# A routed expert stage on one core: the weight splits of a small tile's expert moved into the full tile ahead of it

## The chip, the cores and the metric

The kernel runs on one core of one Trainium2 chip. The metric is the device time of one execution in microseconds, the median of several runs; three runs of the kernel before stand below. One more execution was taken with the hardware profiler, and every row shown here is from that one.

## The reference

Attention, a gated feed-forward layer, and then a layer of eight experts of which each token uses one. The change touches the last layer alone:

```python
N, D, E, F = 896, 768, 8, 1024
logits = x @ w_gate + modality_bias[modality_id]
e_idx = np.argmax(logits, axis=1)
...
for e in range(E):
    mask = e_idx == e
    if not mask.any():
        continue
    h = np.maximum(x[mask] @ w1[e], 0.0)
    out[mask] = gate_w[mask, None] * (h @ w2[e])
```

With the inputs of the test, three experts get tokens: expert 2 has 463, expert 6 has 406 and expert 0 has 27.

## The kernel before

The experts' layer works through tiles of 128 token slots, numbered L from 0. Which expert a tile belongs to is computed on the chip, so the program holds for each tile L of 3 and above two bodies in an If with an Else: `tiny` for an expert's remainder of few tokens, and `full`. Tiles of 7 and above stand inside a further If on the count of tiles. Here the tiles are: 0 to 3 expert 2, all full; 4 expert 6, tiny with 22 tokens; 5 to 7 expert 6, full; 8 expert 0, tiny with 27 tokens; then the end.

`full` computes with weights that are split into a high and a low part (`ra`, made from the raw weights `r1f` of w1 and `r2f` of w2, which lies in the buffer `fa`). One chunk of a split is a cast on ACT (the high part: L795 for w1, L801 for w2) and a subtraction on DVE (the low part: L796 and L802). There are 6 chunks for w1 and 8 for w2. `mm1` (L838) is the product with w1, in two halves of 512 columns, and L915 the product with w2 (called mm2 here). `tiny` reads the raw weights: its product with w1 is L938 and that with w2 is L964, with transposes (L831, L950) and copies (L952) between.

While a tile runs, it prepares what is two tiles ahead: `onehots` (L723, L727 and seven times L731, on DVE) makes the matrices P, seven small matmuls (L744) and some small DVE operations (L746 to L760) turn these into row indices, and `gather` (L807, GpSimd) brings the rows. Rows that an index puts out of range are skipped. Each tile ends with a scaling by the gate, half on ACT and half on DVE (L924 and L925 in `full`, L971 and L972 in `tiny`), and a scatter of the rows (L927, L973).

When the next tile belongs to a new expert, `switch_w1(L)` at the end of tile L, in an If on the register flag_next, splits w1 and the first four chunks of w2, and issues the load of the w1 of the expert after that into `r1f` (a DMA with a condition, on SP). `switch_w2` in the middle of a full tile splits the other four chunks and loads `r2f`. For an expert that begins with a tiny tile, flag_next is set at that tiny tile: here at tile 4, for expert 6. The flags are rows of an integer tile `regs`; a register load (L785, a TENSOR_LOAD) stands on each engine that takes part in an If. Every engine runs the branches, each over its own list of instructions.

Engines take their instructions in program order. Nothing in this part is ordered by a table: the order is that of the code.

Of the kernel before, what the change touches and what calls it, by code (L numbers as in the profile page):

```python
# [458 lines left out]
class Route:  # L459
    def __init__(self, nc, tc, args, k, pool):  # L460
        self.nc, self.tc, self.a, self.k = nc, tc, args, k
        self.p = pool
        t = lambda n, s, d=F32: pool.tile(s, d, name=n)
        self.bsel = t("bsel", [128, NT7, E8])
        self.oh = t("oh", [128, NT7, E8])
        self.ohb = t("ohb", [128, NT7, E8], BF16)
        self.R = t("R", [128, NT7 + 1, E8], BF16)
        self.sums = t("sums", [128, NT7])
        self.rank = t("rank", [128, NT7])
        self.cols = t("cols", [128, NT7, 5], BF16)  # L470
        self.slot = t("slot", [128, NT7])
        self.regp = t("regp", [128, 1], I32)
        self.regs = t("regs", [128, 80], I32)
        self.idx = t("idx", [128, 16], I32)
        self.idxg = t("idxg", [128, 16], I32)
        self.idc = t("idc", [128, 16], I32)
        self.gate = t("gate", [128, 16])
        self.e0 = t("e0", [128, E8])
        self.c0 = t("c0", [128, 2])
        self.trib = t("trib", [128, 128], BF16)  # L480
        self.lgs = {}
        self.oneb = t("oneb", [128, 128], BF16)
# [169 lines left out]
    def flags(self, wk):  # L652
        nc, k = self.nc, self.k
        V = nc.vector
        w = lambda n, s: wk.tile(s, F32, name=n)
        n, gt, nt, base = self.fin
        rf = w("rf", [128, 80])
        V.memset(rf, 0.0)
        pos, act, ev = w("pos", [128, E8]), w("act", [128, E8]), w("ev", [128, E8])
        nact = w("nact", [128, 1])  # L660
        er = k[:, C_E:C_E + E8]
        V.tensor_reduce(out=rf[:, 0:1], in_=nt, op=ALU.add, axis=AX.X)
        V.tensor_scalar(out=rf[:, 0:1], in0=rf[:, 0:1], scalar1=2.0, scalar2=None, op0=ALU.add)
        V.tensor_reduce(out=pos, in_=gt, op=ALU.add, axis=AX.X)
        V.tensor_scalar(out=act, in0=n, scalar1=0.0, scalar2=None, op0=ALU.is_gt)
        V.tensor_tensor(out=ev, in0=act, in1=self.e0, op=ALU.mult)
        V.tensor_tensor(out=act, in0=act, in1=ev, op=ALU.subtract)
        V.tensor_reduce(out=nact, in_=act, op=ALU.add, axis=AX.X)
        V.scalar_tensor_tensor(out=ev, in0=pos, scalar=1.0, in1=er, op0=ALU.is_equal, op1=ALU.mult,
                               accum_out=rf[:, 1:2])  # L670
        V.tensor_scalar(out=rf[:, 2:3], in0=nact, scalar1=0.5, scalar2=None, op0=ALU.is_gt)
        V.tensor_copy(self.regs[:, 0:3], rf[:, 0:3])
        self.fl = (rf, pos, act, nact)
        v1 = self.tiny
        sT = [128, NL - TINY0, E8]
        Lt = k[:, C_L + TINY0:C_L + NL].unsqueeze(2).to_broadcast(sT)
        qa = w("qa", sT)
        self.ts = ts = w("ts", [128, NL])
        V.tensor_tensor(out=qa, in0=base.unsqueeze(1).to_broadcast(sT), in1=Lt, op=ALU.is_equal)
        V.tensor_tensor(out=qa, in0=qa, in1=v1.unsqueeze(1).to_broadcast(sT), op=ALU.mult)  # L680
        V.tensor_reduce(out=ts[:, TINY0:], in_=qa, op=ALU.add, axis=AX.X)
        V.tensor_copy(rf[:, 64 + TINY0:64 + NL], ts[:, TINY0:])

    def flags2(self, wk):
        nc, k = self.nc, self.k
        V = nc.vector
        w = lambda n, s: wk.tile(s, F32, name=n)
        n, gt, nt, base = self.fin
        rf, pos, act, nact = self.fl
        er = k[:, C_E:C_E + E8]  # L690
        sL = [128, NL, E8]
        Lr = k[:, C_L:C_L + NL].unsqueeze(2).to_broadcast(sL)
        bb = base.unsqueeze(1).to_broadcast(sL)
        ab = act.unsqueeze(1).to_broadcast(sL)
        q, q2, kc, kn = w("q", sL), w("q2", sL), w("kc", [128, NL]), w("kn", [128, NL])
        v1 = self.tiny
        bs, bn = w("bs", [128, E8]), w("bn", [128, E8])
        V.tensor_tensor(out=bs, in0=base, in1=v1, op=ALU.add)
        V.tensor_tensor(out=bn, in0=nt, in1=v1, op=ALU.is_gt)
        V.tensor_tensor(out=bn, in0=bn, in1=act, op=ALU.mult)  # L700
        V.tensor_tensor(out=q, in0=bs.unsqueeze(1).to_broadcast(sL), in1=Lr, op=ALU.is_equal)
        V.tensor_tensor(out=q, in0=q, in1=bn.unsqueeze(1).to_broadcast(sL), op=ALU.mult)
        V.tensor_reduce(out=rf[:, 16:16 + NL], in_=q, op=ALU.add, axis=AX.X)
        V.tensor_tensor(out=q2, in0=bb, in1=Lr, op=ALU.is_le)
        V.tensor_tensor(out=q2, in0=q2, in1=ab, op=ALU.mult)
        V.tensor_reduce(out=kc, in_=q2, op=ALU.add, axis=AX.X)
        V.tensor_scalar(out=kn, in0=kc, scalar1=1.0, scalar2=None, op0=ALU.add)
        V.tensor_tensor(out=q, in0=pos.unsqueeze(1).to_broadcast(sL), in1=kn.unsqueeze(2).to_broadcast(sL),
                        op=ALU.is_equal)
        V.tensor_tensor(out=q, in0=q, in1=er.unsqueeze(1).to_broadcast(sL), op=ALU.mult)  # L710
        V.tensor_reduce(out=rf[:, 32:32 + NL], in_=q, op=ALU.add, axis=AX.X)
        V.tensor_scalar(out=rf[:, 48:48 + NL], in0=kc, scalar1=nact[:, 0:1], scalar2=None, op0=ALU.is_lt)
        V.tensor_copy(self.regs[:, 16:64 + NL], rf[:, 16:64 + NL])

    def onehots(self, L, wk, part):
        nc, k = self.nc, self.k
# [21 lines left out]
    def index_first(self, wk, pp, name="px"):  # L738
        nc = self.nc
        V = nc.vector  # L740
        L, nt, P = self.P
        ps = pp.tile([128, 512], F32, name=name)
        for t in range(nt):
            nc.tensor.matmul(ps[:, :5], P[:, t], self.cols[:, t], start=(t == 0), stop=(t == nt - 1))  # L744
        s = wk.tile([128, 8], F32, name="ixs", bufs=2)
        V.tensor_copy(s[:, 0:5], ps[:, :5])  # L746
        V.scalar_tensor_tensor(out=s[:, 5:6], in0=s[:, 0:1], scalar=4096.0, in1=s[:, 1:2], op0=ALU.add, op1=ALU.add)  # L747
        V.tensor_scalar(out=self.idc[:, L:L + 1], in0=s[:, 5:6], scalar1=float(NTOK - 1), scalar2=None, op0=ALU.min)
        return L, s

    def index_rest(self, Ls):
# [11 lines left out]
class Moe2:  # L763
# [93 lines left out]
        nc.vector.tensor_tensor(out=lo, in0=v, in1=hi.bitcast(F32), op=ALU.subtract)  # L857
        self.hhl[hf] = (hi, lo)

    def fetch(self, raw, name, L, lf=None):  # L860
        if lf is None:
            lf = self.val(self.R.regs, 48 + L, 1, self.SP)
        e = self.val(self.R.regs, 32 + L, E8 - 1, self.SP)
        self.nc.sync.dma_start(raw, self.src(name, e), cond=lf, cond_hint=True)

    def switch_w2(self, L):
        with self.tc.If(self.flag > 0):
            for c in range(4, NFC):
                self.split_w2(self.r2f[:, c], c)
            self.fetch(self.r2f, "w2", L)  # L870

    def switch_w1(self, L):
        if L >= 1 and L + 1 < NL:
            with self.tc.If(self.flag_next > 0):  # L874
                for c in range(ND):
                    self.split_w1(self.r1f[:, c], c, 0, 2)
                self.fetch(self.r1f, "w1", L + 1)
            with self.tc.If(self.flag_next > 0):
                for c in range(4):
                    self.split_w2(self.r2f[:, c], c)  # L880
# [6 lines left out]
    def full(self, L, call):  # L887
# [5 lines left out]
        ps = [self.ph.tile([128, 512], F32, name="ph") for _ in range(2)]  # L893
        self.mm1(ps[0], 0, 0, 5)
        call("mid0")
        self.mm1(ps[0], 0, 5, ND)
        self.relu(ps[0], 0)
        call("mid1")
# [32 lines left out]
    def tiny(self, L, G):  # L931
# [29 lines left out]
        for c in range(C):  # L961
            for k in range(G):
                for g in range(G):
                    nc.tensor.matmul(y[W * g:W * g + W, 0:D2], ht[:, c, W * k:W * k + W],  # L964
                                     self.r2f[:, C * k + c, D2 * g:D2 * g + D2],
                                     start=(c == 0 and k == 0), stop=(c == C - 1 and k == G - 1))
        self.fetch(self.r2f, "w2", L, self.flag)
        self.switch_w1(L)
        yo = wk.tile([128, DM], F32, name="ysb", bufs=2)
        o = D2 // 2  # L970
        nc.scalar.activation(yo[:, 0:o], y[:, 0:o], AF.Copy, scale=R.gate[:, L:L + 1])  # L971
# [4 lines left out]
            in_offset=None, bounds_check=G * NTOK - 1, oob_is_err=False)  # L976

    def load_flag(self, L):
        self.flag_next = self.val(self.R.regs, 16 + L + 1, 1)

    def body(self, L, hooks):
        tc, R = self.tc, self.R
        call = lambda name: hooks.get((L, name), lambda: None)()
        more = L + 1 < NL
        if L >= 2 and more:
            self.load_flag(L)
        if L < TINY0:
            self.full(L, call)
        else:
            sm = self.val(R.regs, 64 + L, 1)  # L990
            with tc.If(sm > 0) as cmp:
                self.tiny(L, 4)
            with cmp.Else():
                self.full(L, call)
        call("end")
        if more:
            if L >= 1:
                self.flag = self.flag_next
            if L + 1 < NT7:
                self.body(L + 1, hooks)  # L1000
            else:
# [7 lines left out]
def build(nc, tc, a):  # L1009
    with ExitStack() as es0:  # L1010
# [246 lines left out]
        def mid3_1():  # L1257
# [4 lines left out]
            e = M.val(R.regs, 14, E8 - 1, M.SP)  # L1262
            nc.sync.dma_start(M.r2f, M.src("w2", e), cond=has, cond_hint=True)

        def end1():
            M.NT = M.val(R.regs, 0, NL)
        hooks = {(0, "start"): start0, (0, "mid1"): mid1, (0, "mid2"): mid2, (0, "mm2"): mm2, (0, "mid3"): mid3,
                 (1, "mid0"): mid0_1, (1, "mid2"): lambda: R.onehots(3, wk, False), (1, "mm2"): lambda: R.flags2(wk), (1, "mid3"): mid3_1, (1, "end"): end1}
        M.body(0, hooks)


# [63 lines left out]
```

## Time and profile before

| what | value |
| --- | --- |
| median of 3 runs | 627.27 us (626.29 to 630.08) |
| profiled execution | 626.63 us, of which the span of the profile is 624.9 us |
| TensorE busy | 96% of the span |
| DVE, ACT, GpSimd busy | 67%, 37%, 23% of the span |
| mean granted TensorE clock | 0.985 of full speed |

A busy share counts instructions that occupy the engine; branches, register loads and DMA issues count as idle time. The experts' layer takes the last part of the span: tile 3's second half, tile 4 and the first part of tile 5 lie between 530 and 560 us, and the last tile ends near 616 us.

### The profile page before, as it was taken

What the parts mean: (1) busy time and instruction counts of PE and PEld (TensorE: products, weight loads), DVE (VectorE), ACT (ScalarE), POOL (GpSimd) and SP (SyncE); (2) the same over time, 40 slices, a digit from 0 to 9 for tenths busy, and PEclk for the clock granted to TensorE, in tenths of its full rate; (3) what the DMA queues carried; (4) which work ended last, traced back from release to release, by engine and by line L of the source; (5) the groups of instructions that cost most, each with busy time, mean ns of one, the idle gap of its engine ahead of it and who ended that gap; (6) DMA issues with size and microseconds to landing.
All of it is one profiled execution on the core that took longest, in us unless ns stands there. A gap on an engine that the chain in (4) does not pass through costs nothing. (4 is left out here: it accounts for less than half of the span.)

```text
span 624.9 us, 16865 instructions
## 1 busy us (share of the span) xinstructions
PE 598.6 (96%) x6843; PEld 497.7 (80%) x6843; DVE 416.1 (67%) x993; ACT 234.0 (37%) x544; POOL 143.4 (23%) x243
## 2 busy tenths in 40 slices
PE   8789999999999999999999999999999999979993
PEld 3346666666778999999999979999998888769982
DVE  4478787878856878777777555987759833593322
ACT  4376676766652211111111252212364222361221
POOL 3477666767700000000000015000100101101101
PEclk9799999999999999999999999999999999979998
DMA  7677638656322654444455003310490661156102
GB/s 225 177 193 189 187 114 206 177 180 171 119 64 72 231 188 167 152 152 160 171 178 201 0 1 116 140 50 26 175 335 1 252 254 53 48 225 259 48 31 66
DMA packets 38178, 89.89 MB, mean 144 GB/s; under 512 B 12208, under 2 KB 15596, under 8 KB 38076
## 3 DMA queue, kind: packets, MB, share of 16 engines
q1 hardware_dynamic: 24060, 64.60, 30.7%
q0 software_dynamic: 14016, 23.95, 13.0%
q8 instruction: 62, 1.02, 0.7%
q14 instruction: 40, 0.33, 0.2%
HBM read 69.88 MB, written 5.70 MB: 121 GB/s over the span
## 5 line engine op out<-in xcount | busy, mean ns | idle before, releaser
L111 POOL DMA_DIRECT2D G<-S x156 | 92.2, 609 | 18.9 <-issue 7.8
L1131 PE MATMUL y<-ra,gh 128*128 128x384 f32 x324 | 70.6, 340 | 0.0
L392 ACT CAST whi<-wdec 128x768 fp32r<-128x768 f32 x24 | 20.0, 835 | 124.2 <-DVE wdec L376 116.9
L139 ACT ACTIVATE e<-t,st 124x448 f32<-124x448 f32 x90 | 56.2, 633 | 15.1 <-DVE st L130 15.1
L838 PE MATMUL ph<-ra,xsh 128*128 128x512 f32 x168 | 54.9, 409 | 5.0 <-ACT ra L801 4.5
L130 DVE TENSOR_REDUCE st<-t 124x1 f32<-124x448 f32 x90 | 52.1, 619 | 11.2 <-PE t L122 8.4
L165 PEld LDWEIGHTS o<-Wp,e 60*56 60x56 f32 (+1 forms) x2880 | 48.2, 132 | 13.7 <-issue 12.5
L1131 PEld LDWEIGHTS y<-ra,gh 128*128 128x128 f32 x324 | 56.8, 188 | 0.6 <-issue 0.3
L122 PE MATMUL t<-G,wpre 60*64 60x448 f32 x360 | 53.4, 555 | 3.9 <-DMA G<-S 3.6
L165 PE MATMUL o<-Wp,e 60*56 60x60 f32 (+1 forms) x2880 | 54.0, 221 | 2.4 <-issue 1.4
L189 PEld LDWEIGHTS v<-A2T,vt 120*64 120x64 f32 x672 | 33.6, 136 | 26.6 <-DVE st L148 18.3
L1107 POOL TENSOR_TENSOR ra<-wo,ra 128x768 fp32r<-128x768 f32 x4 | 10.6, 2673 | 191.5 <-ACT ra L1106 191.5
L915 PE MATMUL py<-ra,gh 128*128 128x384 f32 x224 | 49.2, 342 | 0.0
L90 PE MATMUL s<-Kt,Q 64*64 64x448 f32 (+2 forms) x336 | 45.6, 551 | 0.6 <-ACT S L96 0.6
L807 POOL DMA_INDIRECT fa<-yd,idc x11 | 11.5, 1049 | 145.1 <-DVEq L874 64.3
L189 PE MATMUL v<-A2T,vt 120*64 120x120 f32 (+1 forms) x672 | 42.3, 269 | 0.2 <-DVE xl L207 0.2
L177 DVE COPY A2T<-o 120x480 f32<-120x480 f32 (+1 forms) x46 | 30.9, 671 | 16.0 <-PE o L165 15.8
L1131 PE MATMUL y<-ra,gl 128*128 128x384 f32 x162 | 41.3, 336 | 0.0
L838 PEld LDWEIGHTS ph<-ra,xsh 128*128 128x128 f32 x168 | 31.8, 195 | 11.6 <-ACT ra L801 4.9
L915 PEld LDWEIGHTS py<-ra,gh 128*128 128x128 f32 x224 | 38.8, 188 | 1.0 <-issue 1.0
L393 DVE TENSOR_TENSOR wlo<-wdec,whi 128x768 fp32r<-128x768 f32 x24 | 23.0, 958 | 22.4 <-ACT whi L392 22.3
L122 PEld LDWEIGHTS t<-G,wpre 60*64 60x64 f32 x360 | 20.6, 136 | 20.9 <-issue 6.4
(248 smaller groups left out, 1236.2 us busy)
## 6 DMA issues: line engine op xcount, KB each, us to landing
wraw<-in_wab_dram SPq DMA_DIRECT2D x48, 384.0 KB
G<-S POOLq DMA_DIRECT2D x156, 105.0 KB, 3.9
fa<-in_w_dram SPq DMA_DIRECT2D x4, 3072.0 KB
wor<-in_w_out_dram SPq DMA_DIRECT2D x12, 768.0 KB
r1f<-in_w_dram SPq DMA_DIRECT2D x2, 3072.0 KB
r1f<-in_wg_dram SPq DMA_DIRECT2D x8, 384.0 KB
r1f<-in_w_dram SPq DMA_DIRECT2D x4, 768.0 KB
fa<-in_w_dram SPq DMA_DIRECT2D x4, 768.0 KB
```

Of the source, the lines that this page charges most:

```text
L90: nc.tensor.matmul(ps[r][64 * h:64 * h + m, :S], q[64 * r:64 * r + 64, p * 2 * hw + h * hw:p * 2 * hw + h * hw + m], k[64 * r:64 * r + 64, ...
L111: (self.nc.sync if r == 0 and (h == 0 and self.on_sp[n] or n < 2) else self.nc.gpsimd).dma_start(g[64 * r:64 * r + GK, h, :], self.S[blk][ ...
L122: nc.tensor.matmul(t[r][64 * h:64 * h + 64, :S], w[64 * r:64 * r + GK, :], g[64 * r:64 * r + GK, h, :], start=True, stop=True)
L130: self.nc.vector.tensor_reduce(out=st[:124, r:r + 1], in_=self.T[n][r][:124, :S], op=ALU.max, axis=AX.X, negate=True)
L139: self.nc.scalar.activation(e[:124, r, :], t[r][:124, :S], AF.Exp, bias=st[:124, r:r + 1], scale=1.0, accum_out=st[:124, 2 + r:3 + r])
L165: nc.tensor.matmul(o[h][64 * u:64 * u + m, c0:c0 + GK], e[64 * h:64 * h + GK, r, x:x + m], wp[64 * h:64 * h + GK, r, :], start=True, stop= ...
L177: (nc.scalar.copy if h == 0 else nc.vector.tensor_copy)(dst, src)
L189: nc.tensor.matmul(ps[u * 64:(u + 1) * 64, i * w:(i + 1) * w], self.vt[b, p][:, j, u, :], at[:, j * H + 2 * p + u, :w], start=(j == 0), st ...
L393: lambda: V.tensor_tensor(out=lo, in0=x3, in1=hi.bitcast(F32), op=ALU.subtract)]
L838: nc.tensor.matmul(ps, x[:, d], self.w1[:, hf, s, d], start=(d == 0 and i == 0), stop=(d == ND - 1 and i == 2))
L915: nc.tensor.matmul(y[q][:, :384], hx[:, f % 4], self.w2[:, f, s, q * 384:(q + 1) * 384], start=(f == 0 and i == 0), stop=(f == NFC - 1 and ...
L1131: nc.tensor.matmul(y[q][:, :384], gx[:, f % 6], wov[:, f, s, 384 * q:384 * (q + 1)], start=(t > 0 and f == 0 and i == 0), stop=(f == NF - ...
```

## The change

Two rows are added to `regs`: 80 + L says that tile L is an expert's first tile, tiny or not, and that the expert has a full tile; 96 + L is the product of the old flag row 16 + L and row 48 + L (there is a next expert to load). `flag_next` is now row 80, so the full tile ahead of an expert's tiny tile runs the splits, and the tiny tile runs none; the tiny tile issues only the load of `r1f`, under row 96, and no load of `r2f`. The register loads move: `load_flag` from the head of every tile into `full` behind five of the six chunks of mm1's first half, and the small-tile flags of tiles 3 to 7 are loaded once, in tile 2. For tiles of 7 and above, the index of a tile that does not exist is put out of range with the new column `past`.

```diff
@@ flags2
-        V.tensor_copy(self.regs[:, 16:64 + NL], rf[:, 16:64 + NL])
+        V.tensor_tensor(out=q2, in0=bb, in1=Lr, op=ALU.is_equal)
+        V.tensor_tensor(out=q2, in0=q2, in1=bn.unsqueeze(1).to_broadcast(sL), op=ALU.mult)
+        V.tensor_reduce(out=rf[:, 80:80 + NL], in_=q2, op=ALU.add, axis=AX.X)
+        V.tensor_tensor(out=rf[:, 96:96 + NL], in0=rf[:, 16:16 + NL], in1=rf[:, 48:48 + NL], op=ALU.mult)
+        V.tensor_copy(self.regs[:, 16:96 + NL], rf[:, 16:96 + NL])
+        V.tensor_scalar(out=self.past, in0=k[:, C_L:C_L + NL], scalar1=rf[:, 0:1], scalar2=8192.0, op0=ALU.is_ge,
+                        op1=ALU.mult)
...
@@ index_first
+            V.tensor_scalar(out=self.idc[:, L:L + 1], in0=s[:, 5:6], scalar1=float(NTOK - 1),
+                            scalar2=self.past[:, L:L + 1], op0=ALU.min, op1=ALU.max)
...
@@ switch_w1
                 for c in range(ND):
                     self.split_w1(self.r1f[:, c], c, 0, 2)
-                self.fetch(self.r1f, "w1", L + 1)
+                self.fetch(self.r1f, "w1", L + 1, 96)
...
@@ full
         call("mid0")
+        if L >= 2:
+            self.load_flag(L)
         self.mm1(ps[0], 0, 5, ND)
...
@@ tiny
-        self.fetch(self.r2f, "w2", L, self.flag)
-        self.switch_w1(L)
+        if L + 1 < NL:
+            self.fetch(self.r1f, "w1", L + 1, 96)
...
     def load_flag(self, L):
-        self.flag_next = self.val(self.R.regs, 16 + L + 1, 1)
+        if L >= 2:
+            self.flag = self.val(self.R.regs, 16 + L, 1)
+        if L + 1 < NL:
+            self.flag_next = self.val(self.R.regs, 80 + L + 1, 1)
...
@@ body
-        if L >= 2 and more:
-            self.load_flag(L)
...
-            sm = self.val(R.regs, 64 + L, 1)
-            with tc.If(sm > 0) as cmp:
+            with tc.If(self.small[L] > 0) as cmp:
...
+        for i, at in enumerate(("start", "mid1", "mid2", "mm2", "mid3")):
+            hooks[2, at] = lambda i=i: M.load_small(TINY0 + i)
```

The splits stood in both bodies' code before and stand in `full` alone now, so what moves shows in the row of instructions that an engine runs over tiles 3 and 4. On DVE, before, from the end of the full body of tile 3 (its Ifs L874 and L878 are not taken there, so L796 and L802 of this stretch are passed over) into the tiny body of tile 4, up to the copies of the hidden rows:

```order
L796 TENSOR_TENSOR ra<-r1f,ra 128x2x512 [waits Activation_49] x5
...
L802 TENSOR_TENSOR ra<-fa,ra 128x768 [waits Activation_49] x3
...
L925 TENSOR_SCALAR ysb<-py,gate 128x384 [waits DMASW1_49,PE_49]
L991 UNCONDITIONAL_BRANCH
L785 TENSOR_LOAD regs x2
L991 COMPARE_AND_BRANCH
L723 TENSOR_SCALAR rel<-slot 128x7
L727 SCALAR_TENSOR_TENSOR fa<-fa,ts,kc 128x128
L731 TENSOR_SCALAR P<-fa,rel 128x128 [waits DVE_49]
L731 TENSOR_SCALAR P<-fa,rel 128x128 x6
L952 COPY fa<-pt 128x128 [waits PE_49] x2
```

The tiny body of tile 4 then went on, and had these further down, taken here:

```order
L760 TENSOR_TENSOR gate<-ixs 128x1 [waits DVE_49]
L874 COMPARE_AND_BRANCH
L796 TENSOR_TENSOR ra<-r1f,ra 128x2x512 [waits DMAHW5_49,DMAHW3_49,DMAHW7_49,DMAHW1_49,Activation_49]
L796 TENSOR_TENSOR ra<-r1f,ra 128x2x512 [waits Activation_49] x5
L874 UNCONDITIONAL_BRANCH
L874 UNCONDITIONAL_BRANCH [waits DVE_49]
L878 COMPARE_AND_BRANCH
L802 TENSOR_TENSOR ra<-fa,ra 128x768 [waits DMAHW0_49,Activation_49]
L802 TENSOR_TENSOR ra<-fa,ra 128x768 [waits Activation_49] x3
L878 UNCONDITIONAL_BRANCH
L878 UNCONDITIONAL_BRANCH [waits DVE_49]
L972 TENSOR_SCALAR ysb<-py,gate 128x96 [waits DMASW3_49,Activation_49]
```

Now the same engine and place; the Ifs L884 and L888 of tile 3 are taken, and L964 is the copy that was L952:

```order
L807 TENSOR_TENSOR ra<-r1f,ra 128x2x512 [waits Activation_49] x5
...
L813 TENSOR_TENSOR ra<-fa,ra 128x768 [waits Activation_49] x3
...
L937 TENSOR_SCALAR ysb<-py,gate 128x384 [waits DMASW1_49,PE_49]
L1008 UNCONDITIONAL_BRANCH
L1008 COMPARE_AND_BRANCH
L730 TENSOR_SCALAR rel<-slot 128x7
L734 SCALAR_TENSOR_TENSOR fa<-fa,ts,kc 128x128
L738 TENSOR_SCALAR P<-fa,rel 128x128 [waits DVE_49]
L738 TENSOR_SCALAR P<-fa,rel 128x128 x6
L964 COPY fa<-pt 128x128 [waits PE_49] x2
```

What moved: ten subtractions that the program ran behind the tiny tile's copies now stand ahead of them, and ahead of the scaling and the one-hots too.

On PE, before, from the w2 product of tile 4's tiny body to its jump over the Else; behind that jump the next rows run are the two register loads and the branch of tile 5 (`L785 TENSOR_LOAD regs x2`, `L991 COMPARE_AND_BRANCH`):

```order
L964 MATMUL py<-fa 32x192 [waits DVE_49]
L964 MATMUL py<-fa 32x192 x15
L874 COMPARE_AND_BRANCH
L874 UNCONDITIONAL_BRANCH x2
L878 COMPARE_AND_BRANCH
L878 UNCONDITIONAL_BRANCH x2
L991 UNCONDITIONAL_BRANCH
```

Now, with the end of the Else and the branch of tile 5 behind it (the row of dots is the Else, which the jump passes over):

```order
L976 MATMUL py<-fa 32x192 [waits DVE_49]
L976 MATMUL py<-fa 32x192 x15
L1008 UNCONDITIONAL_BRANCH [waits PE_sequencer_49]
...
L1008 UNCONDITIONAL_BRANCH
L1008 COMPARE_AND_BRANCH
```

What moved: the two Ifs of the splits and the two register loads are gone from between the product and the branch; the jump over the Else and the branch over tile 5's tiny body stay.

On SP, the load of `r1f` at the end of tile 3's full body, before (row L864, passed over in tile 3) and now (L874, inside the If that is taken; its condition row 96 is zero there, so that it moves nothing, but it is issued). Before:

```order
L874 COMPARE_AND_BRANCH
L785 TENSOR_LOAD regs x2
L864 ISA
L864 DMA r1f<-in_w_dram 128x6x1024 [waits DMAHW5_49,DMAHW3_49,DMAHW7_49,DMAHW1_49,DVE_49]
L874 UNCONDITIONAL_BRANCH
```

Now, with the tiny body's load, which is new, further down:

```order
L884 COMPARE_AND_BRANCH
L796 TENSOR_LOAD regs x2
L874 ISA
L874 DMA r1f<-in_w_dram 128x6x1024 [waits DMAHW5_49,DMAHW3_49,DMAHW7_49,DMAHW1_49,DVE_49]
L884 UNCONDITIONAL_BRANCH
...
L874 DMA r1f<-in_w_dram 128x6x1024 [waits DMAHW3_49,DMAHW1_49,DMAHW5_49,DMAHW0_49,DMAHW6_49,DVE_49,DMAHW7_49,PE_49,Activation_49]
```

What moved: the same DMA, with its wait for DVE (the last subtraction of w1), is now issued ahead of tile 4. The first matmul of the tiny body (L938, now L950) reads `r1f`, and its semaphores include that of this DMA (DMAHW7) in both programs.

## Rows read from the trace of the kernel before

**Rows 1.** PE's timeline, 537 to 552 us: start, us, engine, line, operation, count, idle before.

```profile
539.08 2.80 PE L938 MATMUL ph<-r1f,fa 128*32 128x256 f32 x48
...
543.18 2.81 PE L964 MATMUL py<-fa 128*32 128x192 f32 x64
550.49 1.19 PE L838 MATMUL ph<-ra,xsh 128*128 128x512 f32 x2 [4.51 <-ACT ra L801]
```

**Rows 2.** PE's sequencer at L991 (tiles 3, 4's end, 5) and L785: ns min/median/max, starts.

```profile
L991 PEldq COMPARE_BRANCH  x1: 2201/2201/2201, 518.1 to 518.1; - x1
...
L991 PEldq COMPARE_BRANCH  x1: 293/293/293, 545.6 to 545.6; - x1
L785 PEldq TENSOR_LOAD <-regs x2: 301/309/317, 545.9 to 546.3; - x2
L991 PEldq COMPARE_BRANCH  x1: 3603/3603/3603, 546.7 to 546.7; - x1
```

**Rows 3.** DMA by queue, 546.5 to 550.5 us: packets, MB, share of 16 engines.

```profile
q8 instruction: 1, 0.02, 1.6%
```

**Rows 4.** DVE's timeline, 534 to 556 us.

```profile
535.88 0.16 DVE L760 TENSOR_TENSOR gate<-ixs 128x1 f32<-128x1 f32 x1
539.19 0.62 DVE L925 TENSOR_SCALAR ysb<-py,gate 128x384 f32<-128x384 f32 x1 [3.15 <-PE py L915]
540.09 0.17 DVE L723 TENSOR_SCALAR rel<-slot 128x7 f32<-128x7 f32 x1 [0.27 <-issue]
540.16 0.34 DVE L727 SCALAR_TENSOR_TENSOR fa<-fa,ts,kc 128x128 f32<-128x128 f32 x1
540.54 1.59 DVE L731 TENSOR_SCALAR P<-fa,rel 128x128 bf16<-128x128 f32 x7
542.83 0.49 DVE L952 COPY fa<-pt 128x128 f32<-128x128 f32 x2 [0.70 <-PE pt L950]
...
545.44 6.90 DVE L796 TENSOR_TENSOR ra<-r1f,ra 128x1024 fp32r<-128x1024 f32 x6 [0.15 <-issue]
552.25 3.56 DVE L802 TENSOR_TENSOR ra<-fa,ra 128x768 fp32r<-128x768 f32 x4
```

**Rows 5.** ACT's timeline, 528 to 553 us.

```profile
539.02 0.58 ACT L924 ACTIVATE ysb<-py,gate 128x384 f32<-128x384 f32 x1 [7.43 <-PE py L915]
...
543.45 5.80 ACT L795 CAST ra<-r1f 128x1024 fp32r<-128x1024 f32 x6
```

**Rows 6.** Windows of 1 us: sum, then busy of PE, PEld, DVE, ACT, POOL, PEclk, DMA, GB/s.

```profile
548.00:549.00 1.00, 0.00 (x0) 0.00 (x0) 1.00 (x2) 1.00 (x2) 0.00 (x0) 0.57 0.10 25
549.00:550.00 1.00, 0.00 (x0) 0.00 (x0) 1.00 (x2) 1.00 (x3) 0.00 (x0) 0.50 0.00 0
...
555.00:556.00 1.00, 1.00 (x6) 0.82 (x5) 1.00 (x3) 0.00 (x0) 0.00 (x0) 1.00 1.01 401
```

**Rows 7.** The chain of waits, at the start of tiles 5 and 6: start, us, what.

```profile
550.49 8.52 PE ph L838 x27
...
571.32 6.18 PE ph L838 x27
```

**Rows 8.** PE's timeline at the start of tile 3.

```profile
520.32 0.73 PE L838 MATMUL ph<-ra,xsh 128*128 128x512 f32 x2 [0.47 <-ACT ysb L924]
```

**Rows 9.** SP's conditional loads of w2 that moved nothing: ns min/median/max, starts.

```profile
L864 SPq DMA_DIRECT2D fa<-in_w_dram x3: 84/99/378, 546.2 to 615.4; - x3
```

**Rows 10.** DVE in flags2, tile 1.

```profile
496.37 0.29 DVE L708 TENSOR_TENSOR q<-pos,kn 128x128 f32<-128x128 f32 x1
```

**Rows 11.** The tail, from several views: branch, scatter, landings (issues' last number), drain.

```profile
L1002 PEldq COMPARE_BRANCH  x1: 6060/6060/6060, 615.6 to 615.6; - x1
616.22 1.00 POOL L973 DMA_INDIRECT out_dram<-ysb,idxg  x1 [1.50 <-DVE ysb L972]
fa<-yd,idc POOLq DMA_INDIRECT x1, 5.5
out_dram<-ysb,idxg POOLq DMA_INDIRECT x1, 5.2
L1330 POOLq DRAIN x3: 52/107/1698, 622.3 to 624.6; - x3
```

More of the change, by code (lines that the diff above doesn't have):

```diff
@@ L472, in __init__ @@
         self.regp = t("regp", [128, 1], I32)
-        self.regs = t("regs", [128, 80], I32)
+        self.regs = t("regs", [128, 112], I32)
+        self.past = t("past", [128, NL])
         self.idx = t("idx", [128, 16], I32)
@@ L656, in flags @@
         n, gt, nt, base = self.fin
-        rf = w("rf", [128, 80])
+        rf = w("rf", [128, 112])
         V.memset(rf, 0.0)
@@ L747, in index_first @@
         V.scalar_tensor_tensor(out=s[:, 5:6], in0=s[:, 0:1], scalar=4096.0, in1=s[:, 1:2], op0=ALU.add, op1=ALU.add)
-        V.tensor_scalar(out=self.idc[:, L:L + 1], in0=s[:, 5:6], scalar1=float(NTOK - 1), scalar2=None, op0=ALU.min)
+        if L < NT7:
+            V.tensor_scalar(out=self.idc[:, L:L + 1], in0=s[:, 5:6], scalar1=float(NTOK - 1), scalar2=None, op0=ALU.min)
+        else:
+            V.tensor_scalar(out=self.idc[:, L:L + 1], in0=s[:, 5:6], scalar1=float(NTOK - 1),
+                            scalar2=self.past[:, L:L + 1], op0=ALU.min, op1=ALU.max)
         return L, s
@@ L858, in transpose_h, with fetch @@
         self.hhl[hf] = (hi, lo)
-    def fetch(self, raw, name, L, lf=None):
-        if lf is None:
-            lf = self.val(self.R.regs, 48 + L, 1, self.SP)
+    def fetch(self, raw, name, L, col):
+        lf = self.val(self.R.regs, col + L, 1, self.SP)
         e = self.val(self.R.regs, 32 + L, E8 - 1, self.SP)
@@ L869, in switch_w2 @@
                 self.split_w2(self.r2f[:, c], c)
-            self.fetch(self.r2f, "w2", L)
+            self.fetch(self.r2f, "w2", L, 48)
     def switch_w1(self, L):
@@ L978, in load_flag, with load_small @@
     def load_flag(self, L):
-        self.flag_next = self.val(self.R.regs, 16 + L + 1, 1)
+        if L >= 2:
+            self.flag = self.val(self.R.regs, 16 + L, 1)
+        if L + 1 < NL:
+            self.flag_next = self.val(self.R.regs, 80 + L + 1, 1)
+    def load_small(self, L):
+        self.small[L] = self.val(self.R.regs, 64 + L, 1)
     def body(self, L, hooks):
@@ L984, in body @@
         more = L + 1 < NL
-        if L >= 2 and more:
-            self.load_flag(L)
+        if L >= NT7 + 1:
+            self.load_small(L)
         if L < TINY0:
@@ L996, in body @@
         if more:
-            if L >= 1:
-                self.flag = self.flag_next
             if L + 1 < NT7:
@@ L1263, in mid3_1 @@
             nc.sync.dma_start(M.r2f, M.src("w2", e), cond=has, cond_hint=True)
+        M.small = {}
         def end1():
```

## The prediction

> **What bounds the kernel now.** I read the page's busy shares first: TensorE is busy for 96% of the span, so only its gaps and its slow stretches are left to win. The costliest product of the last layer, mm1, shows a gap of 4.51 us ahead of tile 5, put down to ACT's split L801 [rows 1]. That gap is what this change bears on, so I read three engines through it on their timelines. PE ends the tiny tile's w2 product at 543.18 + 2.81 = 545.99 and starts tile 5's mm1 at 550.49 [rows 1]. ACT and DVE make the splits meanwhile: the casts of w1 from 543.45, the subtractions from 545.44 to 552.3, then w2's [rows 4, 5]. By this alone PE waits for splits. But a chunk of mm1 needs only its own two parts, and the first pair was there at 545.44 + 6.90/6 = 546.6, four microseconds before PE started. So the last wait to end is another one. The rows of PE's own sequencer name it [rows 2]: the jump over tile 4's Else at 545.6 (0.29 us), two register loads (0.3 us each), and then the branch over tile 5's tiny body, which starts at 546.7 and lasts **3.60 us**, to 550.33. PE starts 0.16 us behind it. A packet of the instruction queue q8, 16 KB and the only one, lies inside that stretch [rows 3]; it is PE's code being brought.
>
> The same branch ahead of tile 3 lasted 2.20 us; there most of it lay beside matmuls in flight, and PE lost 0.47 us [rows 2, 8].
>
> The gap has a second price. While PE stood still the granted clock fell to 0.50, at about 548; it was back at 1.00 in the window from 555, with mm1 running again since 550.49 [rows 6]. [...] The 27 matmuls of mm1's first stretch took 8.52 us in tile 5 and 6.18 us in tile 6 [rows 7]: 2.34 us lost.
>
> [...]
>
> **The change, part by part.**
>
> *The ten subtractions, moved ahead of the tiny tile.* In tile 3 DVE is through with its index work at 535.88 + 0.16 = 536.04 and then idle for 3.15 us, until mm2 ends [rows 4]; ACT is idle for 7.43 us [rows 5]. That idle time is the cover, and for ACT it is enough: six casts are 5.80 us, and the rest of the w2 casts ends before DVE does. DVE is not covered: its work is 6.90 (w1) + 3.56 (w2) = 10.46 us in 3.15 us of room. Engines run in order, so behind these stand tile 3's scaling (0.62), the one-hots (0.17 + 0.34 + 1.59) and the copies of the hidden rows (0.49) [rows 4], on which the tiny tile's w2 product waits. The chain: 536.04 + 0.15 + 10.46 + 0.62 + 2.05 (from 540.09 to 542.13) + 0.49 = 549.8, if branches between them cost nothing; up to 550.5 if each of five costs what 0.15 us of idle shows. The w2 product thus starts at about 549.75 and not at 543.18: **+6.55 us** (to +7.2). It ends at 549.75 + 2.81 = 552.55.
>
> *The first product of the tiny tile.* It reads r1f, into which the skipped load of tile 3 would write, and waits for it; that load waits on SP for the last subtraction of w1, at 536.2 + 6.9 = 543.1. So PE stands from 539.1 to about 543.3, and tile 3's scatter on GpSimd waits for the scaling until some 547.3; nobody needs it soon. A load that moved nothing took 0.1 us to issue [rows 9]; when its semaphore comes no row shows. It is bounded by 0.1 us and by the 5.5 us of a transfer that moves rows [rows 11]; I take the first, since no data moves. With it the product runs 543.3 to 546.1 at full clock, or to 548.9 at half, and with about a microsecond of transposes (542.83 less 541.88) it is in time either way. At 5.5 it would be 2 us late.
>
> *From the tiny tile to tile 5.* The two register loads and their gaps, 546.72 less 545.85 = 0.87 us, go from between the jump and the branch. Does the branch stay? PE's list of instructions around it is the same: what left it are some rows of Ifs and loads, against hundreds that the two jumps pass over. I take it at 3.60 us. The jump came 0.43 us ahead of the end of the product (545.56 against 545.99): now at 552.1, +0.29, +3.60, +0.16 gives mm1 at 556.2, against 550.49: +5.7. If the code had been asked for already at the first jump, the time from there counts, 550.33 less 545.85 = 4.48 us, and mm1 starts at 557.0: +6.5. I take the middle, **+6.1 us**.
>
> The clock falls again, since PE stops for 3.7 us and more, so the 2.34 us stay lost: no term. An added one is possible: PE also stands for 4 us ahead of the tiny tile, nearly as long as in the gap in which the clock fell, and may run its first product, and then the w2 product, at half clock; the latter would take up to 2.81 more. No row shows whether the first product's matmuls bring the clock back by 549.75, as mm1's did by 555. I take 0, since that product is dense too, and keep +2.8 as the bound.
>
> *Tile 3's start.* Two loads fewer stand ahead of its branch. The gap is 0.47 us [rows 8]; between 0 and −0.47, since code that is being brought doesn't come faster for it: **−0.2**.
>
> *Loads of flags inside full tiles.* Each is 0.3 us on a sequencer, two a tile, with fifteen matmuls of 6.18/27 = 0.23 us issued ahead of them: 3.4 us of cover on PE; none. Without that cover, 0.6 us a tile. The flags2 additions are five small operations on DVE, at most 0.29 each [rows 10], 1.4 us, in a tile where every engine's wait for the flags comes later: none.
>
> *The fetch of the next w1* is issued behind the tiny tile's first product, at 546 to 549, and is needed in tile 5's middle; the landing is well ahead: none.
>
> *The tail.* The gather for a tile that doesn't exist took 5.5 us to land, ahead of the last scatter, which took 5.2 from 616.22, to 621.4; then GpSimd's drain of 1.70 us ends near the end of the span [rows 11]. With all its rows out of range the scatter lands some 2 us sooner. But PE's branch out of the nest lasts 6.06 us from 615.6, to 621.7, and the other engines' likewise [rows 11]; they and the drain hold most of it. Bounds 0 and −2, **−0.8**.
>
> Sum: +6.1 − 0.2 − 0.8 = **+5.1 us**. On the profiled execution, 626.63, this is 631.7; it stands 0.64 below the median, 627.27, so the median becomes **632.4 us**, 0.8% slower. A measurement of this kernel can tell about 1% from no change, 6.3 us.
>
> **The rivals.**
>
> *A, PE did wait for the splits.* The page's releaser says so [rows 1], and the change is then a gain at that place: mm1 starts 0.5 us behind the tiny tile's product. But the product itself is still 6.55 us later: +6.55 − 4.51 + 0.5 = +2.5, less the 2.34 of the clock that no longer falls there, less 1.0: −0.8, 626.4 us. Against it stands the finished first pair at 546.6.
>
> *B, the branch gets short.* A jump that finds its code lasted 0.29 us [rows 2]. The end is the same as A's with 0.3 + 0.3 us of branches: 626 to 629 us. For it speaks only that more time passes in tile 4 for code to come; against it, that the target lies as many rows away as before. [...]
>
> *C, slower by over 1%: the first stop costs the clock.* PE's stop of 4.2 us ahead of the tiny tile brings the half clock, and the w2 product still runs at it: up to +2.8 on the sum, 634 to 635.2 us. It decides if that stop lowers the clock and the tiny tile's first product doesn't bring it back by 549.75. A late semaphore of the skipped load (+2) has the same end.
>
> *D, faster by over 1%: the subtractions are hidden.* That needs the one-hots and copies ahead of them on DVE, or DVE done within its 3.15 us. The gap and the clock would go: −4.5 + 0.5 − 2.3 − 1 = −7.3, 620 us. The order of DVE's rows all but excludes it.
>
> **How the numbers follow.** The forecast, 630.5 to 634, has 0.60; C 0.20; A and B together 0.15; D 0.04; the remainder is for something unseen. The range reaches from A and B's upper half to C's end with the late semaphore: 627.5 to 636.5. The 1% bounds are 621.0 and 633.5. Faster: 0.04. Slower: C and the upper part of the forecast (late code, branches on DVE), 0.36. Same: 0.60.
>
> **What the new profile would show.** DVE without a gap from 536 to about 549.7; PE idle for some 4 us ahead of the tiny tile's first product, released by a DMA of SP, and again ahead of its w2 product, released by DVE's copies; a PE branch of 3.6 us or more ahead of tile 5 although the splits were done before; mm1's first stretch in tile 5 at 0.50 clock again, near 8.5 us; the last scatter landing sooner. The forecast is wrong if that branch is short, if the clock stays down across the w2 product, or if the gap ahead of tile 5 closes because the splits are early.

## The result, and the profile after

The changed kernel takes **637.06 us** in the median of six runs (633.22 to 639.59), against 627.22 us for the kernel before in six. The ratio is **1.0145, interval 1.0115 to 1.0174**: slower by 9.1 us (7.2 to 10.9). The profiled execution took 633.22 us with a span of 631.3 us. It is the fastest of the six; e8 below shows where the spread arises.

PE's timeline of the changed kernel, around tile 4 (line numbers moved: L950 was L938, L976 was L964, L849 was L838):

```profile
542.91 4.48 PE L950 MATMUL ph<-r1f,fa 128*32 128x256 f32 x48 [4.19 <-DMA r1f<-in_w_dram]
...
548.85 2.81 PE L976 MATMUL py<-fa 128*32 128x192 f32 x64
557.37 1.19 PE L849 MATMUL ph<-ra,xsh 128*128 128x512 f32 x2 [5.71 <-issue]
```

Where one gap of 4.51 us stood [rows 1], there are two: 4.19 us ahead of the tiny tile's first product, put down to the DMA that moves nothing, and 5.71 us ahead of tile 5. The view calls the second "issue": no engine is named any more, because the splits are long done. DVE's timeline shows what stands ahead of the tiny tile now:

```profile
535.69 6.98 DVE L807 TENSOR_TENSOR ra<-r1f,ra 128x1024 fp32r<-128x1024 f32 x6
542.59 3.55 DVE L813 TENSOR_TENSOR ra<-fa,ra 128x768 fp32r<-128x768 f32 x4
546.07 0.60 DVE L937 TENSOR_SCALAR ysb<-py,gate 128x384 f32<-128x384 f32 x1
...
548.52 0.61 DVE L964 COPY fa<-pt 128x128 f32<-128x128 f32 x2
```

There is no idle time from 535.7 to 548.5; the rows of before [rows 4] had the same instructions with 3.15 us of idle time between, and the ten subtractions behind the copies. Next come the two branches of PE's sequencer (over tile 4's Else and over tile 5's tiny body). Behind them stand SP's two issues of the load of w1: the first, at 542.7, moves nothing (from 542.5 to 547.5 the trace has one packet, 0.02 MB of the instruction queue), the second, at 547.6, moves 3 MB.

```profile
L1008 PEldq COMPARE_BRANCH  x2: 292/3234/6177, 550.7 to 551.0; - x2
```

```profile
L874 SPq DMA_DIRECT2D r1f<-in_w_dram x2: 99/244/388, 542.7 to 547.6; - x2
```

The long branch is still there [rows 2], and went from 3.60 to **6.18 us**. The windows (the last three columns are the granted clock, the share of the DMA engines and GB/s) show the clock and the load:

```profile
546.00:547.00 1.00, 1.00 (x16) 0.53 (x8) 1.00 (x4) 0.00 (x0) 0.00 (x0) 0.50 0.00 0
...
550.00:551.00 1.00, 1.00 (x34) 0.79 (x26) 0.93 (x7) 0.00 (x0) 0.66 (x1) 1.00 0.90 332
551.00:552.00 1.00, 0.66 (x18) 0.25 (x8) 0.09 (x1) 0.10 (x1) 0.36 (x1) 1.00 1.02 365
...
556.00:557.00 1.00, 0.00 (x0) 0.00 (x0) 0.00 (x0) 0.00 (x0) 0.82 (x1) 0.50 0.98 379
```

The first product ran at a granted clock of 0.50 from 544 to 547 (4.48 us instead of 2.80), the w2 product at 1.00 (2.81), and mm1 of tile 5 began at 0.50 again. While PE's branch lasts, from 551.0 to 557.2, the share of the DMA engines is 0.93 to 1.09; before, nothing of this load was under way at that time, since it was issued at 552.4. At the end, the last scatter's landing (the last number, us from issue) shows the tail's small gain [rows 11]:

```profile
out_dram<-ysb,idxg POOLq DMA_INDIRECT x1, 4.2
```

To compare executions I read five marks from each trace, in us **from the end of tile 3's products**, so that what lies ahead drops out. The first three columns are the starts of the products named. There is one trace a row; the kernels are those of the experiments below.

| kernel | w2 product of tile 4 | mm1 of tile 5 | mm1 of tile 6 | end of tile 8's w2 product | end of span |
| --- | --- | --- | --- | --- | --- |
| before | 4.02 | 11.34 | 32.00 | 76.01 | 85.70 |
| changed | 10.13 | 18.65 | 38.98 | 83.44 | 92.59 |
| changed, second trace (e8) | 10.74 | 19.32 | 39.76 | 84.24 | 93.38 |
| e1, load later | 10.04 | 15.95 | 37.41 | 81.82 | 90.94 |
| e2, before without splits | 4.03 | 9.22 | 29.40 | 73.38 | 83.63 |
| e3, no subtractions | 4.02 | 12.42 | 33.12 | 77.52 | 87.04 |
| e4, before reordered | 4.02 | 7.82 | 32.17 | 76.16 | 86.08 |
| e5, changed, reordered | 10.13 | 12.87 | 35.26 | 79.70 | 89.10 |
| e6, before, gathers out of range | 4.02 | 11.27 | 32.32 | 76.36 | 85.83 |
| e7, three chunks | 5.28 | 9.25 | 29.09 | 73.40 | 82.93 |
| e9, e5 and load later | 10.74 | 13.48 | 32.30 | 76.76 | 86.38 |
| e10, e7 and load later | 4.29 | 7.38 | 27.86 | 72.20 | 81.62 |
| e11, before, addresses of the change | 4.02 | 11.34 | 32.52 | 76.92 | 86.35 |
| e12, e10 with padded addresses | 4.02 | 7.21 | 27.94 | 71.91 | 81.03 |

The change costs 6.9 us from that mark on (7.7 in the second trace); the rest of the 9.1 arises ahead of it (e11).

### The profile page after: what moved, and what is told of

Its sections match the earlier page's. It is cut to its first block, busy times and chain, and to the rows that moved or that the text cites. A ratio compares the mean times of both kernels' runs of the same rounds, so it can differ in the third digit from the quotient of the medians.

```text
span 631.3 us, 16870 instructions
## 1 busy us (share of the span) xinstructions
PE 601.8 (95%) x6843; PEld 499.5 (79%) x6843; DVE 417.6 (66%) x998; ACT 233.9 (37%) x544; POOL 142.4 (23%) x243
## 5 line engine op out<-in xcount | busy, mean ns | idle before, releaser
L849 PE MATMUL ph<-ra,xsh 128*128 128x512 f32 x168 | 54.7, 407 | 5.7 <-issue 5.7
L849 PEld LDWEIGHTS ph<-ra,xsh 128*128 128x128 f32 x168 | 31.6, 193 | 12.3 <-issue 6.1
```

The costliest lines, as they stand in the source:

```text
L849: nc.tensor.matmul(ps, x[:, d], self.w1[:, hf, s, d], start=(d == 0 and i == 0), stop=(d == ND - 1 and i == 2))
```

## The experiments

**e1: the load of the next w1, later.** In the changed kernel it is issued 3.4 us ahead of PE's long branch. Here tile 5 issues it behind its own load of w2.

```diff
@@ tiny
-        if L + 1 < NL:
-            self.fetch(self.r1f, "w1", L + 1, 96)
@@ switch_w2
             self.fetch(self.r2f, "w2", L, 48)
+            if L > TINY0:
+                self.fetch(self.r1f, "w1", L, 48)
```

> The changed kernel, with the 3 MB load of the next w1 taken out of the tiny tile and issued in the first full tile behind it, after that tile's load of w2. Theory 1 (PE's code fetch waited behind the packets of that load, which is issued in the changed kernel 3 us before PE's branch ahead of tile 5): the branch is 3.3 to 4.3 us instead of 6.18, tile 5 starts 2 to 3 us earlier, and the median is 630 to 633.5 us. Rival (the branch is longer since the two jumps now follow each other at once): the branch stays at 5.5 us or more and the time stays at 634 to 638.

The branch, and PE's start of tile 5:

```profile
L1008 PEldq COMPARE_BRANCH  x2: 293/1938/3584, 556.6 to 557.0; - x2
```

```profile
560.72 1.19 PE L849 MATMUL ph<-ra,xsh 128*128 128x512 f32 x2 [3.10 <-issue]
```

The branch is 3.58 us, as before the change, and the gap 3.10 us instead of 5.71. Median 632.7 us, ratio 1.0082 (1.0059 to 1.0105), against 1.0145 with the change. So the load that the change moved forward lengthened PE's branch, by 2.6 us. That a block of code waited among the load's packets is the expectation's reading; no run here shows how the load did it.

Not all of it stays won. mm1 starts 2.7 us earlier in the table, but the span ends only 1.65 us earlier (2.4 against the second trace of the changed kernel): mm1's first stretch took 9.17 us here and 8.05 in the changed kernel, since the granted clock was still 0.50 in the window from 565, five microseconds into it (in the changed kernel it was 0.63 in the window from 560, three microseconds into it, and 1.00 from 561). The medians, by their ratios, are about 4 us apart, with intervals wide enough for either figure.

**e2: no splits at all.** The kernel before, with the calls behind the tiny tile's w2 product left out.

```diff
@@ tiny
-        self.fetch(self.r2f, "w2", L, self.flag)
-        self.switch_w1(L)
```

> The kernel before, with the splits of expert 6's first weights and the load behind them left out of the tiny tile, so that tiles 5 to 8 compute with wrong weights. Theory 1 (PE waits for its code): the branch ahead of tile 5 stays at 3 to 4.5 us and the gap ahead of tile 5 at 3.5 to 4.5 us, the half clock with it; the time is within 2 us of the kernel before. Rival (PE waits for the splits): the gap falls under 1 us, and the time is 5 to 7 us less.

```profile
551.58 0.71 PE L838 MATMUL ph<-ra,xsh 128*128 128x512 f32 x2 [2.39 <-issue]
```

```profile
L989 PEldq COMPARE_BRANCH  x1: 2202/2202/2202, 549.2 to 549.2; - x1
```

With nothing to wait for, PE still stood for 2.39 us in a branch of 2.20 us, and mm1's first stretch of 27 still took 8.03 us. The one execution took 627.76 us, though its marks end 2.1 us earlier. The gap is less than theory 1 expected, and far from the rival. So 2.39 of the 4.51 us stand without any split; that the splits didn't hold PE up for the rest either, e4 shows. The two Ifs of the splits went as well, and the branch starts right at the product's end (0.7 us behind it before). Why it was 3.60 us before and 2.20 here stays open (before, a gather's transfers move at 546 to 548 us; that they are the cause wasn't tried).

**e3: no subtractions in tile 3.** The changed kernel, with ACT's casts but not DVE's ten instructions there.

```diff
@@ split_w1 (split_w2 likewise; low is False in tile 3's switch_w1 alone)
-        nc.vector.tensor_tensor(out=lo, in0=r, in1=hi.bitcast(F32), op=ALU.subtract)
+        if low:
+            nc.vector.tensor_tensor(out=lo, in0=r, in1=hi.bitcast(F32), op=ALU.subtract)
```

> The changed kernel, with the ten subtractions (low parts of expert 6's w1 and of four chunks of w2) left out in tile 3, so that DVE is free there. Theory 1 (DVE's order delays tile 4): the tiny tile's first product starts within 1 us of the end of tile 3's products, its w2 product starts 5 to 6.5 us earlier than in the changed kernel, and the time falls by 5 to 7 us, to 627 to 631; the branch ahead of tile 5 stays above 5 us, since the load of w1 still lies ahead of it. Rival (what counts is not DVE but the order of flags and loads): the w2 product moves by less than 2 us.

```profile
541.73 2.80 PE L952 MATMUL ph<-r1f,fa 128*32 128x256 f32 x48
...
545.82 2.81 PE L978 MATMUL py<-fa 128*32 128x192 f32 x64
...
554.22 1.19 PE L851 MATMUL ph<-ra,xsh 128*128 128x512 f32 x2 [5.59 <-issue]
```

```profile
L1010 PEldq COMPARE_BRANCH  x2: 293/3175/6057, 547.6 to 548.0; - x2
```

Tile 4 is back where it was (4.02 in the table, against 10.13), and one execution took 630.66 us. The gap ahead of tile 5 stays at 5.59 us, with a branch of 6.06: the load is in front of it as in the changed kernel, and no subtraction is left that PE could wait for. The two costs are separate.

**e4: the long branch taken away.** In the kernel before, the bodies of tiles 5 to 7 change places, so that PE falls through into tile 5 behind one jump.

```diff
@@ body, for tiles 5 to 7
-            with tc.If(sm > 0) as cmp:
-                self.tiny(L, 4)
-            with cmp.Else():
-                self.full(L, call)
+            with tc.If(sm < 1) as cmp:
+                self.full(L, call)
+            with cmp.Else():
+                self.tiny(L, 4)
```

> The kernel before, with the two bodies of tiles 5, 6 and 7 in the other order in the program (full first, tiny in the Else), so that PE falls through into tile 5 behind its jump over tile 4's Else; nothing else changes. Theory 1 (two jumps in a row reach code that isn't there): no branch over 1.5 us ahead of tile 5; mm1 starts at about 547, paced by the subtractions at 1.15 us a chunk, at full clock; the median is 622 to 625 us. Rival (PE waits for the splits): mm1 starts at 550 as before, and the time stays at 626 to 628.

PE's branch into tile 5, then PE's gaps on its timeline, then DVE's:

```profile
L992 PEldq COMPARE_BRANCH  x1: 73/73/73, 548.0 to 548.0; - x1
```

```profile
548.25 0.70 PE L838 MATMUL ph<-ra,xsh 128*128 128x512 f32 x2 [0.99 <-ACT ra L795]
551.39 0.50 PE L838 MATMUL ph<-ra,xsh 128*128 128x512 f32 x1 [0.17 <-DVE ra L796]
...
563.26 1.01 PE L915 MATMUL py<-ra,gl 128*128 128x384 f32 x2 [2.41 <-DVE gl L857]
```

```profile
546.70 6.90 DVE L796 TENSOR_TENSOR ra<-r1f,ra 128x1024 fp32r<-128x1024 f32 x6 [0.15 <-issue]
553.52 3.56 DVE L802 TENSOR_TENSOR ra<-fa,ra 128x768 fp32r<-128x768 f32 x4
...
559.05 3.55 DVE L802 TENSOR_TENSOR ra<-fa,ra 128x768 fp32r<-128x768 f32 x4
562.53 0.68 DVE L857 TENSOR_TENSOR gl<-pt,gh 128x512 fp32r<-128x512 f32 x1
```

One window of the clock, in the columns of above:

```profile
564.00:565.00 1.00, 1.00 (x4) 1.00 (x4) 0.73 (x2) 0.00 (x0) 0.00 (x0) 0.50 0.86 180
```

The long branch is gone: it is 0.07 us, the gap 0.99, mm1 starts 3.5 us sooner and then goes at DVE's pace. The time missed its forecast: ratio 1.0007 (0.9976 to 1.0037). All of it was given back by tile 6 (32.17 against 32.00 in the table), most of it inside tile 5's w2 product: PE waits 2.41 us there for a low part that stands behind 14 us of subtractions on DVE, and then runs at a granted clock of 0.50 until about 566. DVE had been hidden behind the long branch; that is also how the profile's releaser could name the splits. The branch's rows are 3.60 us (before) and 2.20 us (e2) with two jumps, and 0.07 us in e4, where the second branch isn't taken. That PE stands there for its code is my reading: the packet of [rows 3] is one of the instruction queue, and no row says for which engine.

**e5 and e9: the change, reordered; and with the later load.** e5 is the changed kernel with e4's edit, e9 has e1's edit as well.

> The changed kernel, with the same reordering of the bodies of tiles 5, 6 and 7 as in the kernel with the long branch removed. Theory 1 (two costs, DVE's order ahead of tile 4 and the code ahead of tile 5, which add up): the tiny tile's w2 product still starts at 548.5 to 549.5, no branch over 1.5 us stands ahead of tile 5, its mm1 starts 0.5 to 1.5 us behind the product, at full clock and without waits for subtractions; 6 to 8 us less than the changed kernel, 625 to 629. If the load of the next w1 holds back the next block of code as well, a gap of 1 to 4 us appears inside mm1 and the time is 628 to 632. Rival (the reordering is worth nothing, since something else ends last): within 2 us of the changed kernel.

> The changed kernel with both: the bodies of tiles 5 to 7 reordered and the load of the next w1 issued behind tile 5's load of w2. Theory 1 (three costs: DVE's order 6 us, the code 3.6 us and half clock 2.3, the load 2.6 us and its wait on ACT): no long branch, no wait of ACT ahead of tile 5's w2 product; from the end of tile 3's products to the end of the span 85.5 to 86.7 us, against 85.7 before, 92.6 with the change and 89.1 with the reordering alone. Rival (another cost is hidden behind these): above 87.5 us.

In e5 there is no gap ahead of tile 5, but a new one ahead of its w2 product, and ACT's row names the cause:

```profile
567.55 0.71 PE L863 MATMUL pt<-kc,fa 128*128 128x128 f32 x4 [2.88 <-ACT fa L856]
```

```profile
563.70 3.03 ACT L812 CAST ra<-fa 128x768 fp32r<-128x768 f32 x4 [4.04 <-DMA r1f<-in_w_dram]
```

ACT's cast of w2 stands behind a wait for the load of w1. Neither branch of the expectation had that place; median 634.16 us, ratio 1.0096 (1.0058 to 1.0134), above both. In e9 that wait is gone, and the mark at the end is 86.38 us as forecast (85.5 to 86.7), 631.7 us in one execution. So DVE's 6 us, the long branch with a granted clock of 0.50 behind it, and the load, which lengthened PE's branch or held up ACT's cast, account for the experts' tiles.

**e6: gathers out of range alone**, in the kernel before.

> The kernel before, with the gathers of tiles that don't exist put out of range and nothing else. Theory 1: the last scatter lands 4 to 4.5 us after its issue instead of 5.2, and from its issue to the end of the span it takes 7.8 to 8.2 us instead of 8.7; all else as before. Rival (the tail is held by the branch and the drain alone): 8.5 us and more.

8.41 us from the last scatter's issue to the end, between the two. In the traces with gathers in range it is 8.63 (before), 8.85 (e4), 9.18 (e2) and 8.37 (e11); in the others out of range 7.96 to 8.52. The two groups overlap. Their means differ by half a microsecond, which one trace a kernel doesn't settle.

**e8: the changed kernel again.**

> The changed kernel once more, unaltered, for a second trace. Theory 1 (the code ahead of tile 5 waits among the packets of the load of the next w1, which differ from execution to execution): the branch ahead of tile 5 is again over 5 us, but not the same as 6.18 within 0.1; all else from the end of tile 3's products within 0.5 us. If the six times, 633 to 640 us, differ for something ahead of the experts' tiles, then the branch is the same and the tiles start earlier or later.

```profile
L1008 PEldq COMPARE_BRANCH  x2: 293/3265/6237, 555.2 to 555.5; - x2
```

6.24 us: the branch is the same, against my first alternative. The one execution took 637.83 us, 4.6 more than the first trace's, and most of the difference is the arrival: tile 3's products end at 542.63 in this trace and at 538.72 in the first. So the two executions differ mainly ahead of tile 4; what differs there stays open.

The marks are 0.6 to 0.8 us later too, not within the 0.5 that I expected. The first product took 5.35 us here and not 4.48, and the w2 product had to wait for it:

```profile
546.72 5.35 PE L950 MATMUL ph<-r1f,fa 128*32 128x256 f32 x48 [4.09 <-DMA r1f<-in_w_dram]
```

**e7 and e10: a version that uses DVE's idle time.** e7 is the kernel before with e4's edit, the gathers out of range, and the splits divided: three of six chunks of w1 in tile 3, the rest in the tiny tile. e10 has e1's edit and the flags loaded inside the tiles too, and no load of w2 in the tiny tile. Both need wider flags.

```diff
@@ full, end (self.first is flag row 80)
+        with self.tc.If(self.first > 0):
+            for c in range(3):
+                self.split_w1(self.r1f[:, c], c, 0, 2)
@@ switch_w1
-                for c in range(ND):
+                for c in range(3, ND):
                     self.split_w1(self.r1f[:, c], c, 0, 2)
```

> The kernel before with the reordered bodies, the gathers out of range, and three of the six chunks of expert 6's w1 split in tile 3 (3.45 us of subtractions in 3.15 us of DVE's idle time), the other three chunks and those of w2 in the tiny tile as before. Theory 1 (each stall has its own cause, and DVE's idle time in tile 3 is free): the tiny tile's w2 product starts as before, within 0.5 us; mm1 of tile 5 starts within 1.5 us of its end and isn't paced by subtractions; a wait of 1 to 2.5 us for DVE may remain ahead of tile 5's w2 product; 3 to 5.5 us less than before, 622 to 625. Rival (DVE's work is one chain, and what leaves one place waits at the next): the wait ahead of the w2 product grows to 3 us and more, and the time is within 2 us of before.

> The kernel with three chunks split in tile 3 and three in the tiny tile, with the flags loaded inside the tiles as the change does and the load of the next w1 behind tile 5's load of w2. Theory 1: the gap ahead of tile 5 falls from 1.17 us to about 0.4 us, as two register loads go; from the end of tile 3's products to the end of the span 81 to 82.9 us, against 82.9 with the three chunks alone and 85.7 before; the median is 3 to 5 us below before. Rival (code or transfers wait elsewhere in tile 5): above 83.5 us.

e7's two gaps in tile 5, ahead of mm1 and inside the w2 product:

```profile
554.26 0.70 PE L848 MATMUL ph<-ra,xsh 128*128 128x512 f32 x2 [1.17 <-ACT ra L805]
566.07 0.61 PE L927 MATMUL py<-ra,gl 128*128 128x384 f32 x2 [0.86 <-DVE gl L867]
```

Both are near their forecasts, and in e10 the first is 0.28 us. (The tiny tile's w2 product missed its forecast in e7, 5.28, for a gather that landed late.) The marks fell to 82.93 and 81.62, by 2.8 and 4.1 us. But the medians missed theirs: 626.84 (ratio 0.9981, 0.9950 to 1.0013) can't be told from no change, and 626.78 (0.9972, 0.9950 to 0.9993) is 1.8 us down. Something outside these tiles took back about 2 us.

**e11 and e12: addresses.** The kernels with wider flags above had slower products of split values (176.4 to 177.9 ns from start to start, against 175.3 before), in stages that no edit touches. e11 is the kernel before with nothing but the buffers' addresses of the changed kernel; e12 is e10 with a pad.

```diff
@@ e11
-        self.regs = t("regs", [128, 80], I32)
+        self.regs = t("regs", [128, 112], I32)
+        self.past = t("past", [128, NL])
@@ e12
-        self.past = t("past", [128, NL])
+        self.past = t("past", [128, NL + 224])[:, 0:NL]
```

> The kernel before, with the integer tile of the flags 112 columns wide and an unused tile of 16 columns behind it, so that every buffer behind them lies 192 bytes further on, exactly as in the changed kernel; no instruction changes. Theory 2 (the shifted addresses slow the products of split values on PE, in all stages): the mean spacing of the w_out products is 177.9 ns as in all runs of the changed kernel, against 175.3 before, tiles 6 to 8 take 0.4 us more, and the median is 1.5 to 3.5 us above before, which is what of the change's 9 us the experts' tiles don't show. Rival (the changed instructions, the flags or the state of the chip slow them): spacing 175.3 and a time within 1 us of before.

> The kernel with three chunks split in tile 3 and the late load, with the tile behind the flags padded so that every later buffer lies 1024 bytes further on than in the kernel before, in place of 128. Theory 2: the spacing of the w_out products is back at 175.3 to 175.5 ns (177.6 without the pad), and the median falls by another 1.5 to 3 us, to a ratio of 0.990 to 0.995. Rival (another property of the addresses, or none): 177 ns and more, and a ratio of 0.997 as without the pad.

The w_out products from 380 to 440 us, by form; the number behind the comma is the mean ns of one. Before, the changed kernel, e11 and e12:

```profile
L1131 PE MATMUL y<-ra,gh 128*128 128x384 f32 x222 | 48.2, 338 | 0.0
```

```profile
L1146 PE MATMUL y<-ra,gh 128*128 128x384 f32 x220 | 48.0, 340 | 0.0
```

```profile
L1132 PE MATMUL y<-ra,gh 128*128 128x384 f32 x219 | 48.0, 340 | 0.0
```

```profile
L1159 PE MATMUL y<-ra,gh 128*128 128x384 f32 x224 | 48.4, 338 | 0.0
```

These overlap; the mean spacing of the starts of these products (gaps over 0.3 us left out), worked out from the trace, is 175.3, 177.9, 177.9 and 175.1 ns. e11 is slower than before by a ratio of 1.0046 (1.0024 to 1.0069), 2.9 us, of which its marks show 0.65 us behind tile 3. e12 has a median of **623.77 us, ratio 0.9918 (0.9896 to 0.9940)**: faster than both kernels by more than the intervals.

## Why the prediction was right or wrong

The direction was right, by the mechanism of its first term; the size was short. It forecast +5.1 us; measured are +9.1. The median is half a microsecond above the range's upper end; taken by the ratio on the prediction's own base, it is 636.4 us, just inside. That is luck: the upper end was there for rival C with a late semaphore, and neither came. Slower by over 1% had been given 0.36, and no change clear of 1% had 0.60.

Of the 4.0 us that are missing, two terms that the prediction put at nothing or didn't have make up 4.5: the addresses 2.9 us (e11), and the load 1.65 us at the end of the span (e1). The other terms together came out about half a microsecond under their forecast; the intervals are wider than that.

- *The ten subtractions ahead of the tiny tile: right.* Forecast +6.55 us on the w2 product, measured +6.11 (10.13 less 4.02). The first product's wait, forecast 4.2 us behind tile 3's products, was 4.19: the skipped load's semaphore came at once (issued at 542.7, the product started at 542.91). e3 shows that it was DVE.
- *The clock: right.* The first product ran at 0.50 from 544 to 547 and was in time in the first trace; in the second it took 5.35 us, and the w2 product was 0.6 us late (e8). In the first the w2 product ran at 1.00, so rival C's price didn't fall due. mm1's first stretch took 8.05 us in tile 5 and 6.43 in tile 6, so 1.6 us stayed lost rather than 2.34.
- *The branch ahead of tile 5: the cause right, the size wrong.* It stayed though the splits were done, against rivals A, B and D, but at 6.18 us and not between 3.60 and 4.48. The step that failed is the one on the fetch of the next w1, costed at "none" because "the landing is well ahead". I asked who needs its data, and not what else would be under way beside it: e1 shows 2.6 us for PE's branch, of which 1.65 us reach the end. That it would also hold up ACT's cast shows in e5 alone, where PE no longer hides it.
- *Tile 3's start:* the 0.47 us went in the first trace and were 0.43 in the second: nothing to claim. *The tail:* −0.5 us in the marks, forecast −0.8; e6 and e11 leave open how much of it is the gathers. The branch of 6.06 us out of the nest [rows 11] is PE's alone: in the same trace those of the other engines took 38 to 56 ns.
- *A term that was missing, and the larger of the two.* One wider tile and one new one shifted all later buffers by 192 bytes, and e11 prices that alone at 2.9 us (1.5 to 4.3). With 6.9 to 7.7 us from the end of tile 3's products on, of which 0.65 are this too, the sum is 9.2 to 10.0, inside the measured 7.2 to 10.9.

The profile's releaser for the old gap, ACT's split, was the last wait that the profile could name and not the one that ended last; the sequencer's rows had it.

## What to carry to other kernels

When the profile puts a gap down to another engine, read the waiting engine's own sequencer too. In this kernel a branch of 3.60 us there ended last, and earlier data didn't shorten it (6.18 us with the change, 3.58 in e1). Compare work that is to move into an engine's idle time with that idle time; here, in 3.15 us of DVE's, three chunks (3.45 us) fitted and ten (10.46 us) didn't. Before moving a transfer forward, ask what it will run beside, branches included. Before widening a tile, ask what it shifts behind it: e12's pad was worth 0.5%.

## What the runs showed of the hardware that I had not expected

- A 3 MB load under way lengthened PE's branch from 3.58 to 6.18 us (e1 against the changed kernel), and to 6.24 and 6.06 in two more traces (e8, e3).
- The products of split values went at 175.1 to 175.5 ns with buffers shifted by 0, 64 or 1024 bytes against the kernel before, at 176.4 and 177.6 with 128 (e7, e10), and at 177.6 to 177.9 with 192, the same in every trace of the changed kernel and its variants. What property of the address decides is open.
- Between tile 3's products and the end, the two traces of the changed kernel agree within 0.8 us; the end of tile 3's products differs by 3.9 us between them.
